# A routing-attention and bilinear-FFN kernel: weight rounding spread over the first FFN, evictions and sums on other engines, the verdict computed earlier

## The chip, the cores and the metric

The kernel runs on one core of one Trainium2 chip. The metric is the device time of one execution in microseconds (us). Before the change the median of three runs is 1273.95 us (1273.7 to 1275.91).

## The reference, cut to what matters

The inputs are `q`, `k`, `v` of shape (4, 8, 768, 64), `centroids` (8, 16, 64), the weights `moe_w_a` and `moe_w_b` (512, 1536) and `moe_w_out` (1536, 512). The weights are 64-bit floats in memory.

```python
q_assign = argmax(q_n @ c_n)            # per head: nearest of 16 centroids
k_assign = argmax(k_n @ c_n)
mask = q_assign[:, :, :, None] == k_assign[:, :, None, :]
scores = where(mask, 0.125 * q @ k.T, -1e9)
attn = softmax(scores) @ v              # (B, H, S, D) -> x of (B*S, H*D)
out = ((x @ w_a) * (x @ w_b)) @ w_out   # 3072 tokens
```

## The kernel before, in words

**Units.** Heads are taken in 16 pairs (4 batches of 4 pairs). For a pair and a half of its 768 queries (`hf`) there are six units, one for each block of 128 keys (`j` = 0 to 5); a unit is a 128x2x384 tile of scores, the middle index `a` being the head of the pair. Two units make a group, three groups a half, six a pair: 96 groups (`g`) and two more turns of the main loop (L510) to finish.

**A turn of the main loop** writes the instructions of one group in this order, and each engine works its own in that order: `score` (mask matmuls of one-hot codes L381, then scores L390 on PE; exponential L397 on ACT), `add_up` of the group before (running sums of the probabilities, L409, one head on DVE, the other on POOL), `weigh` of the group before (L420, PE), one of six preparation steps for the next pair (`prep_steps`, L347: transposes L282, centroid similarities L298, assignment L309 to L327, one-hot codes L337), rounding of weight parts (`round_w`, L219, then the load of the part after next), pieces of the FFN, and, in every third turn, `denominators` (L431: PE matmul of the finished sums, evicted by ACT L440) or, one turn later, `normalize` (L444: three reciprocals on DVE, the product with `xT` on POOL L452, and a row sum of the reciprocals on ACT L454). The turns with g a multiple of 3 hold `denominators`, those with remainder 1 `normalize`.

**Weight rounding.** 36 parts of 128x512: 24 of `wa` and `wb`, in the order of thirds of 512 columns, then 12 of `wo`. A part takes five DVE operations (L229 to L242), an addition on POOL (L245) and a last DVE operation that waits for it (L247). Before the change 9/8 parts fall on each turn, so that 29 are written by turn 25 and all by turn 31.

**The FFN** of a batch is put into a deque when its last pair is normalised (turns 25, 49, 73, 97). A batch is two blocks of 384 tokens. A block is 24 "up" pieces (L467: eight matmul records; `wa` pieces are evicted by ACT L478, `wb` pieces by a product on DVE L482) and three "down" pieces (L488, 24 records; evicted by ACT L492, stored by SP L495). A credit lets three up pieces into each turn; a down piece costs a third more, so that after three down turns one turn has none. Two blocks take 24 turns. PSUM has three buffers `m` for all preparations, denominators and pieces, two for scores and one for `O`.

**The end.** When all is written, `stat` (sums of denominators and reciprocals) gives a count of rows outside the limits (L118 to L131), all engines load it (L132) and branch: a long path L136 would recompute everything if the count were not zero.

Of the kernel before, what the change touches and what calls it, by code (L numbers as in the profile page):

```python
# [33 lines left out]
def kernel(  # L34
# [75 lines left out]

    stat = const.tile([P, 4 * B * HP], FP32, name="stat")
    with ExitStack() as fast:
        short_path(nc, tc, fast, c, cn, stat, q, k, v, moe_w_a, moe_w_b,
                   moe_w_out, out)

    fine = const.tile([P, 4 * B * HP], FP32)  # L118
    nc.vector.tensor_scalar(out=fine, in0=stat, scalar1=LIMIT, scalar2=None,
                            op0=ALU.is_le)  # L120
    least = const.tile([P, 1], FP32)
    nc.vector.tensor_reduce(out=least, in_=fine, axis=AX.X, op=ALU.min)
    far_off = const.tile([P, 1], FP32)
    nc.vector.tensor_scalar(out=far_off, in0=least, scalar1=-1.0, scalar2=1.0,
                            op0=ALU.mult, op1=ALU.add)
    n_far = const.tile([1, 1], INT32)
    with tc.tile_pool(name="ps_e", bufs=1, space=PS) as ps_e:
        ps = ps_e.tile([1, 1], FP32, name="e")
        nc.tensor.matmul(out=ps, lhsT=far_off, rhs=ones[:, 0:1], start=True,
                         stop=True)  # L130
        nc.vector.tensor_copy(out=n_far, in_=ps)  # L131
    redo = nc.values_load(n_far[0:1, 0:1], min_val=0, max_val=P,  # L132
# [5 lines left out]

def short_path(nc, tc, ctx, c, cn, stat, q, k, v, moe_w_a, moe_w_b, moe_w_out,
               out):  # L140
# [28 lines left out]
    hap = pool("hap", 2)  # L169
# [84 lines left out]
    ohs = []
    for n in range(2):
        t = zero.tile([P, 4 * 3, P], BF16, name=f"oh{n}")
        nc.gpsimd.memset(t, 0.0)
        ohs.append(t)

# [16 lines left out]
    def prep_transpose(p, i):  # L276
# [9 lines left out]
        dst = qkTs[p][:, i * 512:(i + 1) * 512]  # L286
        if i == 1:
            nc.vector.tensor_copy(out=dst, in_=ps)
        else:
            nc.scalar.copy(out=dst, in_=ps)  # L290

    def prep_sim(p):


        hp = p % HP
        ps = ps_m.tile([P, 512], FP32, name="m")
        for kq in range(4):
# [4 lines left out]
        t = simp.tile([P, HB], FP32, name="simT")  # L302
        nc.scalar.copy(out=t, in_=ps[:, 0:HB])  # L303
        sims[p] = t

    def prep_assign(p):
        ps = ps_m.tile([P, 512], FP32, name="m")
        for t in range(3):
# [6 lines left out]
        nc.vector.tensor_reduce(out=mx, in_=sim, axis=AX.X, op=ALU.max)  # L315
        eq = simp.tile([P, NG, NC], FP32, name="eq")
        nc.vector.tensor_tensor(
            out=eq, in0=sim, in1=mx[:, :, None].broadcast_to((P, NG, NC)),
            op=ALU.is_ge)
        rk = simp.tile([P, NG, NC], FP32, name="rk")  # L320
        nc.vector.tensor_tensor(
            out=rk, in0=eq, in1=rank[:, None, :].broadcast_to((P, NG, NC)),
            op=ALU.mult)
        first = small.tile([P, NG], FP32, name="first")
        nc.vector.tensor_reduce(out=first, in_=rk, axis=AX.X, op=ALU.max)
        oh = ohs[p % 2].rearrange("p n (a e) -> p (n a) e", a=2)
        nc.vector.tensor_tensor(  # L327
# [3 lines left out]
    def prep_onehot(p, w):  # L331
# [3 lines left out]
        for n in range(NJ):  # L335
            kq, t = divmod(n, 3)
            nc.tensor.transpose(out=ps[:, n * P:(n + 1) * P],  # L337
                                in_=ohs[p % 2][:, 4 * t + 2 * w + kq, :],
                                identity=identb)
# [61 lines left out]
    def add_up(u):  # L401
# [57 lines left out]

    def ffn_block(b, blk):  # L460
        box = {}
        t0 = blk * HB
# [33 lines left out]

        for f in range(NF):
            ffn.append((NCH * HB, lambda f=f: piece_a(f)))
            ffn.append((NCH * HB, lambda f=f: piece_b(f)))
        for n in range(3):  # L500
            ffn.append((NF * DM, lambda n=n: down(n)))

# [6 lines left out]

    for step in prep_steps(0):  # L510
        step()
    for g in range(NG + 2):
# [259 lines left out]
```

## Time and profile before

| | us |
|---|---|
| median of three runs | 1273.95 |
| the profiled execution | 1274.98 |
| its span, first to last instruction | 1273.1 |
| PE busy (modelled) | 1166.8 |
| DVE busy | 449.4 |
| ACT busy | 297.8 |
| POOL busy | 262.9 |

Times of rows count from the start of the span. Busy PE is modelled, since matmuls are pipelined; idle time of an engine costs only where something on the path waits for it.

### The profile page before, as it was taken

How to read it: one execution, taken by the hardware profiler on the slowest of the kernel's cores; microseconds unless marked ns; L12 is line 12 of the kernel's file. 1: busy time of each engine (PE TensorE's matmuls, PEld its weight loads, DVE VectorE, ACT ScalarE, POOL GpSimd, SP SyncE). 2: the span in 40 equal slices, each digit the busy share in tenths (PEclk: the TensorE clock that was granted, in tenths of full speed). 3: DMA queues.
4: the chain of work that ended last, by engine and by line, in shares of the span. 5: the costliest groups of instructions: out<-in, count | busy, mean ns of one | idle time of the engine just before them, and what ended most of it. 6: DMA issues, size and time to landing. Idle time of an engine off the chain costs nothing.

```text
span 1273.1 us, 11938 instructions
## 1 busy us (share of the span) xinstructions
PE 1166.8 (92%) x4723; PEld 579.6 (46%) x4723; DVE 449.4 (35%) x697; ACT 297.8 (23%) x542; POOL 262.9 (21%) x238
## 2 busy tenths in 40 slices
PE   6556555899999999999999999999999999999997
PEld 3222222355445554455445544455445544554553
DVE  5888888775312241322313140322313130110110
ACT  4223233222222322222222222222222221100000
POOL 2444343433202222221111121221111130000000
PEclk9788878899999999999999999999999999999999
DMA  6143231321020001100030001100000000000000
GB/s 169 60 120 104 67 104 66 104 75 30 8 64 17 13 1 46 41 3 11 9 78 1 13 1 54 34 13 1 9 17 1 1 1 25 1 1 25 1 1 27
DMA packets 63375, 44.92 MB, mean 35 GB/s; under 512 B 51536, under 2 KB 55632, under 8 KB 63312
## 3 DMA queue, kind: packets, MB, share of 16 engines
q1 hardware_dynamic: 63168, 44.05, 12.5%
q8 instruction: 39, 0.64, 0.2%
q14 instruction: 24, 0.20, 0.1%
q10 hardware_dynamic: 144, 0.03, 0.0%
HBM read 37.78 MB, written 6.29 MB: 35 GB/s over the span
## 4 chain that ended last, share of the span: by engine, by line
PE 82%; DVE 10%; POOL 4%; issue 3%; ACT 0%; DMA 0%; POOLq 0%; DVEq 0%; ACTq 0%
PE m L467 39%; PE m L488 20%; PE O L420 8%; PE s L390 7%; PE s L381 2%; PE m L436 2%; DVE inv L449 2%; DVE acc L409 2%; PE m L282 2%; POOL acc L409 1%; POOL wb_sb L245 1%; POOL wa_sb L245 1%; DVE wb_sb L247 1%; DVE rest L239 1%; DVE wa_sb L247 1%
## 5 line engine op out<-in xcount | busy, mean ns | idle before, releaser
L467 PE MATMUL m<-xT,wa_sb 128*128 128x384 f32 x768 | 265.6, 489 | 0.4 <-ACT simT L303 0.4
L467 PE MATMUL m<-xT,wb_sb 128*128 128x384 f32 x768 | 264.1, 487 | 0.0
L488 PE MATMUL m<-wo_sb,h 128*128 128x512 f32 x576 | 251.6, 594 | 0.0
L482 DVE TENSOR_TENSOR h<-ha,m 128x384 f32<-128x384 f32 x96 | 52.9, 553 | 403.2 <-PE m L467 403.2
L467 PEld LDWEIGHTS m<-xT,wa_sb 128*128 128x128 f32 x768 | 143.8, 190 | 108.4 <-issue 6.0
L467 PEld LDWEIGHTS m<-xT,wb_sb 128*128 128x128 f32 x768 | 144.0, 190 | 96.7 <-issue 0.6
L488 PEld LDWEIGHTS m<-wo_sb,h 128*128 128x128 f32 x576 | 108.0, 190 | 133.5 <-issue 129.4
L397 ACT ACTIVATE pt<-s 128x768 f32<-128x768 f32 x192 | 145.9, 806 | 72.3 <-issue 25.9
L390 PE MATMUL s<-qkT 64*128 64x384 f32 x768 | 154.1, 524 | 0.0
L409 POOL TENSOR_TENSOR acc<-acc,pt 128x384 f32<-128x384 f32 x128 | 141.7, 1107 | 59.5 <-ACT pt L397 53.2
L420 PE MATMUL O<-pt,v 128*64 128x384 f32 x768 | 149.8, 512 | 0.0
L478 ACT COPY ha<-m 128x384 f32<-128x384 f32 x96 | 46.0, 479 | 377.9 <-PE m L467 377.9
L452 POOL TENSOR_TENSOR xT<-xT,inv 128x384 f32<-128x384 f32 x32 | 35.7, 1114 | 440.7 <-DVE inv L449 440.7
L381 PE MATMUL s<-ohT 64*128 64x384 bf16 x384 | 51.9, 347 | 63.8 <-ACT pt L397 21.7
L409 DVE TENSOR_TENSOR acc<-acc,pt 128x384 f32<-128x384 f32 x128 | 97.5, 762 | 15.3 <-ACT pt L397 10.7
L390 PEld LDWEIGHTS s<-qkT 64*128 64x128 f32 x768 | 77.4, 203 | 35.5 <-issue 6.8
L449 DVE RECIPROCAL inv<-den 128x128 f32<-128x128 f32 x96 | 82.2, 912 | 25.9 <-ACT den L440 25.9
L420 PEld LDWEIGHTS O<-pt,v 128*64 128x64 f32 x768 | 48.1, 141 | 94.4 <-issue 90.6
L492 ACT COPY y<-m 128x512 f32<-128x512 f32 x24 | 14.1, 586 | 249.1 <-PE m L488 249.1
L409 POOL TENSOR_TENSOR acc<-pt 128x384 f32<-128x384 f32 x32 | 34.1, 1067 | 168.8 <-ACT pt L397 168.8
L381 PEld LDWEIGHTS <-ohT 64*128 64x128 bf16 x384 | 12.0, 95 | 116.8 <-issue 76.3
L436 PE MATMUL m<-acc,ones 128*64 128x384 f32 x128 | 29.1, 533 | 25.8 <-DVE acc L409 25.8
(76 smaller groups left out, 510.8 us busy)
## 6 DMA issues: line engine op xcount, KB each, us to landing
qk<-in_q_dram SPq DMA_DIRECT2D x32, 192.0 KB, 3.9
qk<-in_k_dram SPq DMA_DIRECT2D x32, 192.0 KB, 4.6
v<-in_v_dram SPq DMA_DIRECT2D x16, 384.0 KB, 4.4
raw<-in_moe_w_a_dram SPq DMA_DIRECT2D x12, 512.0 KB, 3.6
raw<-in_moe_w_b_dram SPq DMA_DIRECT2D x12, 512.0 KB, 3.6
raw<-in_moe_w_out_dram SPq DMA_DIRECT2D x12, 512.0 KB, 3.4
out_dram<-y SPq DMA_DIRECT2D x24, 256.0 KB, 2.0
csb<-in_centroids_dram ACTq DMA_DIRECT2D x1, 32.0 KB, 1.8
```

The costliest lines, as they stand in the source:

```text
L381: nc.tensor.matmul(out=s[:, a, 0:HB], lhsT=ohTs[p][r, S + j * P:S + (j + 1) * P], rhs=ohTs[p][r, hf * HB:(hf + 1) * HB], start=True, stop= ...
L390: nc.tensor.matmul(out=s[:, a, 0:HB], lhsT=qkTs[p][r, S + j * P:S + (j + 1) * P], rhs=qkTs[p][r, hf * HB:(hf + 1) * HB], start=False, stop ...
L397: nc.scalar.activation(out=pt, in_=s[:, :, 0:HB], func=AF.Exp, scale=SCALE)
L409: eng.tensor_tensor(out=acc[:, a, :], in0=probs[u - 1][:, a, :] if j == 1 else acc[:, a, :], in1=probs[u][:, a, :], op=ALU.add)
L420: nc.tensor.matmul(out=O_of[0][a * D:(a + 1) * D, 0:HB], lhsT=vs[p][:, a, j, :], rhs=probs[u][:, a, :], start=(j == 0), stop=(j == NJ - 1))
L436: nc.tensor.matmul(out=ps[a * D:(a + 1) * D, 0:HB], lhsT=ones, rhs=acc[:, a, :], start=True, stop=True)
L449: nc.vector.reciprocal(out=inv[:, n * P:(n + 1) * P], in_=den[:, n * P:(n + 1) * P])
L452: nc.gpsimd.tensor_tensor(out=x, in0=x, in1=inv, op=ALU.mult)
L467: nc.tensor.matmul(out=ps[:, 0:HB], lhsT=w_sb[:, ch, f * P:(f + 1) * P], rhs=xTs[b][:, ch, t0:t0 + HB], start=(ch == 0), stop=(ch == NCH - 1))
L478: nc.scalar.copy(out=box["a"], in_=ps[:, 0:HB])
L482: nc.vector.tensor_tensor(out=box["h"][:, f, :], in0=box["a"], in1=ps[:, 0:HB], op=ALU.mult)
L488: nc.tensor.matmul(out=ps, lhsT=box["h"][:, f, n * P:(n + 1) * P], rhs=wo_sb[:, f, :], start=(f == 0), stop=(f == NF - 1))
```

## The change

Over turns 0 to 23 only eight weight parts are rounded, one in each third turn (2, 5, ..., 23); the other 28 are written in turns 24 to 40, two or one in each (2 2 1 2 1 2 2 1 2 1 2 2 1 2 1 2 2). The FFN of the first batch is reordered to match: eight up pieces of block 0, eight of block 1, for each third of the columns, then the down pieces of both; `h` gets a second buffer. Of the first head's sums, `j` = 2 and 4 move from DVE to POOL. Two evictions of the preparation (the second of three `qkT` tiles, the second one-hot tile) move from DVE to ACT. To find the memory, `qk`, `acc`, `oh` lose their second buffer, `v` its third, and the reciprocal is taken in place in `den`, as is ACT's row sum of it. So the load of the next pair's q and k is written after the transposes, that of v two steps later. An exponential is put among the first ACT instructions. The verdict is computed after the last `normalize`, with its matmul behind the first piece of the last FFN batch; the load of the count and the branch stay at the end.

```diff
+    ce = const.tile([P, 1], FP32)
+    nc.scalar.activation(out=ce, in_=cn0, func=AF.Exp)
...
-    qkp = pool("qkp", 2)
-    vp = pool("vp", 3)
+    qkp = pool("qkp", 1)
+    vp = pool("vp", 2)
...
-    accp = pool("accp", 2)
+    accp = pool("accp", 1)
...
-    hp_ = pool("hp", 1)
+    hp_ = pool("hp", 2)
...
-        if i == 1:
-            nc.vector.tensor_copy(out=dst, in_=ps)
-        else:
-            nc.scalar.copy(out=dst, in_=ps)
+        nc.scalar.copy(out=dst, in_=ps)
...
-            nc.vector.tensor_scalar(out=dst, in0=ps[:, 0:S], scalar1=FAR,
-                                    scalar2=-FAR, op0=ALU.mult, op1=ALU.add)
+            nc.scalar.activation(out=dst, in_=ps[:, 0:S], func=AF.Identity,
+                                 scale=FAR, bias=nfar[:, 0:1])
...
-            both(lambda: load(p + 1), lambda: prep_transpose(p, 0)),
-            both(lambda: prep_transpose(p, 1), lambda: prep_transpose(p, 2)),
-            lambda: prep_sim(p),
+            lambda: prep_transpose(p, 0),
+            both(lambda: prep_transpose(p, 1), lambda: prep_transpose(p, 2),
+                 lambda: load(p + 1)),
+            both(lambda: prep_sim(p), lambda: load_v(p)),
...
-        for a, eng in ((0, nc.vector), (1, nc.gpsimd)):
+        for a in range(2):
+            eng = nc.gpsimd if a == 1 or j in (2, 4) else nc.vector
...
-        inv = denp.tile([P, HB], FP32, name="inv")
         for n in range(3):
-            nc.vector.reciprocal(out=inv[:, n * P:(n + 1) * P],
-                                 in_=den[:, n * P:(n + 1) * P])
+            part = den[:, n * P:(n + 1) * P]
+            nc.vector.reciprocal(out=part, in_=part)
         x = xTs[b][:, hp, hf * HB:(hf + 1) * HB]
-        nc.gpsimd.tensor_tensor(out=x, in0=x, in1=inv, op=ALU.mult)
+        nc.gpsimd.tensor_tensor(out=x, in0=x, in1=den, op=ALU.mult)
         n = 4 * p + 2 * hf + 1
-        nc.scalar.activation(out=den, in_=inv, func=AF.Copy,
+        nc.scalar.activation(out=den, in_=den, func=AF.Copy,
                              accum_out=stat[:, n:n + 1])
...
+    def ffn_batch(b):
+        blocks = [ffn_block(b, blk) for blk in range(2)]
+        if b == 0:
+            for n in range(3):
+                for ups, _ in blocks:
+                    ffn.extend(ups[8 * n:8 * n + 8])
+            for _, downs in blocks:
+                ffn.extend(downs)
+        else:
+            for ups, downs in blocks:
+                ffn.extend(ups + downs)
...
+    due = {}
+    for i in range(len(w_parts)):
+        due.setdefault(3 * i + 2 if i < 8 else 24 + int((i - 8) / 1.6),
+                       []).append(i)
...
-        for i in range(g * 9 // 8, (g + 1) * 9 // 8):
+        for i in due.get(g, ()):
             round_w(i)
             load_w(i + 2)
...
+    fine = zero.tile([P, 4 * NPAIR], FP32, name="fine")
+    nc.vector.tensor_scalar(out=fine, in0=stat, scalar1=LIMIT, scalar2=None,
+                            op0=ALU.is_le)
+    least = zero.tile([P, 1], FP32, name="least")
+    nc.vector.tensor_reduce(out=least, in_=fine, axis=AX.X, op=ALU.min)
+    far_off = zero.tile([P, 1], FP32, name="far_off")
+    nc.vector.tensor_scalar(out=far_off, in0=least, scalar1=-1.0, scalar2=1.0,
+                            op0=ALU.mult, op1=ALU.add)
+    ffn.popleft()[1]()
+    ps = ps_m.tile([P, 512], FP32, name="m")
+    nc.tensor.matmul(out=ps[0:1, 0:1], lhsT=far_off, rhs=ones[:, 0:1],
+                     start=True, stop=True)
+    nc.vector.tensor_copy(out=n_far, in_=ps[0:1, 0:1])
     while ffn:
         ffn.popleft()[1]()
```

## Rows read from the trace of the kernel before

**Rows 1.** Page, part 2: PE's busy tenths in 40 equal slices; its granted clock.

```profile
PE   6556555899999999999999999999999999999997
...
PEclk9788878899999999999999999999999999999999
```

**Rows 2.** Windows: stretch, its length, busy us (instructions) by engine, clock, DMA.

```profile
18.00:236.00 218.00, 128.94 (x696) 56.54 (x696) 175.26 (x260) 62.95 (x108) 92.30 (x76) 0.81 0.33 93
236.00:520.00 284.00, 283.56 (x1173) 140.39 (x1172) 104.30 (x164) 73.00 (x134) 63.36 (x56) 1.00 0.12 34
```

**Rows 3.** Timeline (start, us, engine, line, operation): first PE instructions of turns 0, 13, 14, 26, 28; a stall in turn 26.

```profile
18.13 0.82 PE L381 MATMUL s<-ohT 64*128 64x384 bf16 x4 [0.65 <-DVE ohT L344]
...
121.74 0.50 PE L381 MATMUL s<-ohT 64*128 64x384 bf16 x4
...
125.93 0.50 PE L381 MATMUL s<-ohT 64*128 64x384 bf16 x4
...
236.01 0.50 PE L381 MATMUL s<-ohT 64*128 64x384 bf16 x4
...
245.82 2.85 PE L467 MATMUL m<-xT,wa_sb 128*128 128x384 f32 x8 [0.44 <-ACT simT L303]
...
260.92 0.50 PE L381 MATMUL s<-ohT 64*128 64x384 bf16 x4
```

**Rows 4.** Timeline, 300 to 326 us: one undisturbed rounding, the next one's start; last of five assignment operations.

```profile
300.51 0.44 DVE L229 TENSOR_SCALAR wo_sb<-raw 128x512 int32<-128x512 int32 x1
...
302.94 1.38 POOL L245 TENSOR_TENSOR wo_sb<-wo_sb,rest 128x512 f32<-128x512 f32 x1 [12.72 <-DVE rest L239]
...
304.96 0.42 DVE L229 TENSOR_SCALAR wo_sb<-raw 128x512 int32<-128x512 int32 x1
...
325.96 0.56 DVE L327 TENSOR_TENSOR oh<-rk,first 128x384 bf16<-128x384 f32 x1
```

**Rows 5.** Line L409: additions on POOL and DVE, ns min/median/max.

```profile
L409 POOL TENSOR_TENSOR acc<-acc,pt x128: 985/997/1332, 30.7 to 1057.8; 128x384 f32<-128x384 f32 x128
L409 DVE TENSOR_TENSOR acc<-acc,pt x128: 494/558/1351, 32.2 to 1057.0; 128x384 f32<-128x384 f32 x128
```

**Rows 6.** Timeline around 101 us (DVE, POOL), and line L247, ns min/median/max.

```profile
101.56 1.00 POOL L409 TENSOR_TENSOR acc<-pt 128x384 f32<-128x384 f32 x1
101.64 1.47 DVE L247 SCALAR_TENSOR_TENSOR wa_sb<-ex,wa_sb 128x512 f32<-128x512 int32 x1 [1.17 <-POOL wa_sb L245]
...
L247 DVE SCALAR_TENSOR_TENSOR wo_sb<-ex,wo_sb x12: 691/1080/1474, 210.3 to 308.8; 128x512 f32<-128x512 int32 x12
```

**Rows 7.** Timeline, 1079 to 1084 us: denominators to `xT` with nothing in the way.

```profile
1079.79 0.87 PE L436 MATMUL m<-acc,ones 128*64 128x384 f32 x4
...
1081.47 2.58 DVE L449 RECIPROCAL inv<-den 128x128 f32<-128x128 f32 x3 [23.35 <-ACT den L440]
1083.27 2.74 PE L467 MATMUL m<-xT,wb_sb 128*128 128x384 f32 x8
1084.14 0.52 ACT L454 ACTIVATE den<-inv 128x384 f32<-128x384 f32 x1 [2.77 <-DVE inv L449]
1084.19 0.99 POOL L452 TENSOR_TENSOR xT<-xT,inv 128x384 f32<-128x384 f32 x1 [25.22 <-DVE inv L449]
1084.57 0.18 ACT L454 ACTIVATION_READ_ACCUMULATOR den<-inv 128x1 f32 x1
```

**Rows 8.** Timeline: the exponentials of turn 1.

```profile
23.69 1.51 ACT L397 ACTIVATE pt<-s 128x768 f32<-128x768 f32 x2 [0.50 <-PE s L390]
```

**Rows 9.** Windows around two PE waits (columns as in Rows 2).

```profile
92.00:96.00 4.00, 1.16 (x9) 0.32 (x9) 3.86 (x5) 0.30 (x1) 1.88 (x2) 1.00 0.31 120
...
103.00:113.30 10.30, 0.06 (x2) 0.10 (x1) 8.94 (x15) 2.70 (x5) 3.96 (x4) 0.73 0.19 64
```

**Rows 10.** Timeline: the last instructions of the span.

```profile
1266.57 0.58 ACT L492 COPY y<-m 128x512 f32<-128x512 f32 x1 [9.76 <-PE m L488]
1266.65 0.15 DVE L131 CAST n_far<-e 1x1 int32<-1x1 f32 x1 [29.85 <-PE e L129]
```

More of the change, by code (lines that the diff above doesn't have):

```diff
@@ L109 @@
     nc.gpsimd.memset(cTb, 0.0)
-    stat = const.tile([P, 4 * B * HP], FP32, name="stat")
+    n_far = const.tile([1, 1], INT32, name="n_far")
     with ExitStack() as fast:
-        short_path(nc, tc, fast, c, cn, stat, q, k, v, moe_w_a, moe_w_b,
+        short_path(nc, tc, fast, c, cn, n_far, q, k, v, moe_w_a, moe_w_b,
                    moe_w_out, out)
[L118 to L131, printed above, removed]
     redo = nc.values_load(n_far[0:1, 0:1], min_val=0, max_val=P,
@@ L136, with short_path @@
             long_path(nc, tc, slow, c, q, k, v, out)
-def short_path(nc, tc, ctx, c, cn, stat, q, k, v, moe_w_a, moe_w_b, moe_w_out,
+def short_path(nc, tc, ctx, c, cn, n_far, q, k, v, moe_w_a, moe_w_b, moe_w_out,
                out):
@@ L194, in load, with load_v @@
         qks[p] = t
+    def load_v(p):
+        if p >= NPAIR:
+            return
+        b, hp = divmod(p, HP)
         t = vp.tile([P, 2, NJ, D], FP32, name="v")
@@ L201, in short_path @@
     load(0)
+    load_v(0)
     WN = 512
@@ L251, in short_path @@
     load_w(1)
[L254 to L258, printed above, removed]
+    stat = zero.tile([P, 4 * NPAIR], FP32, name="stat")
+    nfar = zero.tile([P, 1], FP32, name="nfar")
+    nc.vector.memset(nfar, -FAR)
+    oh_all = zero.tile([P, 4 * 3, P], BF16, name="oh")
+    nc.gpsimd.memset(oh_all, 0.0)
     ps = ps_m.tile([P, 512], FP32, name="m")
@@ L301, in prep_sim @@
                              start=True, stop=True)
-        t = simp.tile([P, HB], FP32, name="simT")
+        t = simp.tile([P, HB], FP32, name="sim")
         nc.scalar.copy(out=t, in_=ps[:, 0:HB])
@@ L315, in prep_assign @@
         nc.vector.tensor_reduce(out=mx, in_=sim, axis=AX.X, op=ALU.max)
-        eq = simp.tile([P, NG, NC], FP32, name="eq")
+        rk = simp.tile([P, NG, NC], FP32, name="sim")
         nc.vector.tensor_tensor(
-            out=eq, in0=sim, in1=mx[:, :, None].broadcast_to((P, NG, NC)),
+            out=rk, in0=sim, in1=mx[:, :, None].broadcast_to((P, NG, NC)),
             op=ALU.is_ge)
-        rk = simp.tile([P, NG, NC], FP32, name="rk")
         nc.vector.tensor_tensor(
-            out=rk, in0=eq, in1=rank[:, None, :].broadcast_to((P, NG, NC)),
+            out=rk, in0=rk, in1=rank[:, None, :].broadcast_to((P, NG, NC)),
             op=ALU.mult)
@@ L325, in prep_assign @@
         nc.vector.tensor_reduce(out=first, in_=rk, axis=AX.X, op=ALU.max)
-        oh = ohs[p % 2].rearrange("p n (a e) -> p (n a) e", a=2)
+        oh = oh_all.rearrange("p n (a e) -> p (n a) e", a=2)
         nc.vector.tensor_tensor(
@@ L337, in prep_onehot @@
             nc.tensor.transpose(out=ps[:, n * P:(n + 1) * P],
-                                in_=ohs[p % 2][:, 4 * t + 2 * w + kq, :],
+                                in_=oh_all[:, 4 * t + 2 * w + kq, :],
                                 identity=identb)
@@ L495, in down @@
             nc.sync.dma_start(out=rows, in_=y)
[L497 to L501, printed above, removed]
+        ups = [(NCH * HB, lambda f=f, piece=piece: piece(f))
+               for f in range(NF) for piece in (piece_a, piece_b)]
+        downs = [(NF * DM, lambda n=n: down(n)) for n in range(3)]
+        return ups, downs
+    def ffn_batch(b):
[9 more added lines that the diff above has]
+                ffn.extend(ups + downs)
     GPP = UPP // 2
@@ L508, in short_path @@
     credit = 0
-    for step in prep_steps(0):
-        step()
+    due = {}
+    for i in range(len(w_parts)):
+        due.setdefault(3 * i + 2 if i < 8 else 24 + int((i - 8) / 1.6),
+                       []).append(i)
+    prep_transpose(0, 0)
+    prep_transpose(0, 1)
+    prep_transpose(0, 2)
+    load(1)
+    prep_sim(0)
+    prep_assign(0)
+    prep_onehot(0, 0)
+    prep_onehot(0, 1)
     for g in range(NG + 2):
@@ L542, in short_path @@
             if ph[1] == 1 and ph[0] % HP == HP - 1:
-                for blk in range(2):
-                    ffn_block(ph[0] // HP, blk)
+                ffn_batch(ph[0] // HP)
+    fine = zero.tile([P, 4 * NPAIR], FP32, name="fine")
[11 more added lines that the diff above has]
+    nc.vector.tensor_copy(out=n_far, in_=ps[0:1, 0:1])
     while ffn:
```

## The prediction, made before the change was run

> **What bounds the kernel now.** I read the page's slices first [rows 1]: from slice 9 on PE is busy nine tenths or more at the full clock (2.4 GHz); ahead of that it is busy five or six tenths at a clock between 0.7 and 0.9. The windows by stage say who holds it up there [rows 2]: in 18 to 236 us, turns 0 to 25, DVE is busy 175 of 218 us and PE 129; in 236 to 520 us, two blocks and more of FFN, PE is busy all the time. So only the first stretch has time to give. It lasts from the first score at 18.13 to turn 26's at 236.01, 8.4 us a turn; a turn in which nothing waits takes 4.2 (125.93 - 121.74) [rows 3]. The other end of the scale is 26 x 4.2 = 109 us instead of 218.
>
> An undisturbed rounding takes 304.96 - 300.51 = 4.45 us of DVE, waiting for POOL's 1.38 included [rows 4]. 29 parts stand in the first stretch: 129 us. After the change there are 12, eight of them one in three turns.
>
> **The change part by part.**
>
> *The port that DVE and POOL share.* POOL's addition takes 0.99 undisturbed and up to 1.33, DVE's 0.56 and up to 1.35 [rows 5]; DVE's last rounding operation takes 0.69 alone, and 1.47 when a POOL addition began just before it (101.56 to 102.56, then 0.69 more) [rows 6]. So operations of this kind go one after the other, and a sum moved from DVE to POOL occupies the common resource for 0.99 instead of 0.56. The Trainium skill, "SBUF — State Buffer", "Who interferes with whom", says that a DVE instruction with two SBUF inputs and a GpSimd one that reads SBUF exclude each other completely: the row agrees. That rule speaks against this move; without it the sum would be that of rival 1.
>
> *A half after the change, from one denominators matmul's end to the next.* POOL and DVE now hand the first head's sum back and forth, and the single `acc` ties it to the matmul. Start at 0. ACT evicts; reciprocals end at 3.4, POOL's product at 4.5 (1080.66 to 1084.05 and 1085.18) [rows 7]. Behind it on POOL: `j`=2 of both heads, to 6.5; then DVE's `j`=3 to 7.1, POOL's `j`=3 to 8.2 (port), DVE's first four rounding operations to 10.5, POOL's rounding addition to 12.0, `j`=4 to 13.0, DVE's last rounding operation to 13.7, POOL's `j`=4 to 14.7, DVE's `j`=5 to 15.3, POOL's `j`=5 to 16.3, matmul (0.87) to 17.2. In every second half the assignment (five operations of 0.56 and the gaps, 2.9) [rows 4] stands between `j`=5 and the reciprocals on DVE, of which 2.2 is covered: 17.9. PE's own work is 3 x 4.2 = 12.6 to 13.3, so it waits some 4 us at each denominators matmul. A wait of 2.8 left the clock at 1.00 in 92 to 96 us, one of 10 took it to 0.73 [rows 9]; 4 us lies between. If it falls, PE's three turns become some 16 us, still under 17.2. I take 17.2 and 17.9; bounds are PE's 13.3 and 20 (clock low, every collision lost).
>
> *First stretch.* First score 0.5 later (18.6): the second one-hot eviction now follows the first on ACT. Turn 1's exponentials end at 25.2 + 0.5 [rows 8], `j`=2 can start on POOL, and 12.6 later (17.2 - 4.5) the first denominators are done: 38.4. Seven more halves: 4 x 17.9 + 3 x 17.2 = 123.2, to 161.6; turn 25 takes 4.4: turn 26 starts at 166. Before: 236.0. Gain **70.0**; with all halves at the bounds: at 13.3 the first is done at 34.5 and turn 26 starts at 132, gain 104; at 20 at 186, gain 50.
>
> *Where the stall goes: turns 24 to 27.* Two parts each in the turns 24 and 25, which are still short. DVE from 160: parts 8, 9 to 169, `j`=1, parts 10, 11 to 178.9, reciprocals to 181.5, POOL's product to 182.7, ACT's sum of `den` to 183.4. That last one now reads and writes `den` in place and so waits for POOL's product (it did not before: L454 starts with L452 [rows 7]); on ACT turn 26's exponentials, the `simT` copy and the `wa` eviction are queued behind it, to 185.4. PE reaches the third piece of turn 26 at 166 + 4 + 2 x 2.65 = 175.3 (2.74 a piece, overlapped [rows 7]) and needs `simT`'s PSUM buffer: idle for 10. The same wait exists now, 0.44 long, at the same place (245.82) [rows 3]. In turn 27 its denominators need the buffer of a product that stands behind parts 13 and 14 on DVE, done at 205: another 5. Two turns took 260.92 - 236.01 = 24.9 before; they take some 40 now. **+15**.
>
> *Turns 28 to 40.* A turn there is 12 us of PE. DVE: 1.65 parts x 4.45 = 7.3, sum 0.6, product 0.8, reciprocals or assignment 1.3 on average, 0.8 of collisions: 10.8. It fits, but turns with two parts and reciprocals need 14, so I add **+3** (0 to 20) of waits. Weights are in time: the second third is needed from turn 31 and written by 28, the third from 36 and by 33, `wo` from 42 and by 40. PE's work is the same in any order of pieces. I also take off the 0.8 that turn 26 lost before to the same wait (245.82 against the end of its second piece, and turn 27).
>
> *Later batches.* No rounding left; PE is full [rows 1]. The added POOL sums (0.9 us a turn), ACT copies (0.3 a turn) and the wait of ACT's row sum lie beside 8 us of FFN pieces a turn: 0.
>
> *Loads.* q and k of the next pair are asked for after the transposes, on SP's queue ahead of the weight parts, and are used five turns later, over 20 us; DMA is a third busy in that stretch [rows 2]: 0. If the buffer came late by a turn, PE's transposes would wait, 1 to 2 us a pair. The early exponential takes a table load off a place where ACT waits for PE anyway: 0.
>
> *Verdict.* It moves into PE's stream behind one piece of the last batch. It needs both sums of `stat`. Before, PE starts that batch at once, at 1080.6, and its first piece ends at 1083.3 [rows 7]. The reciprocals end at 1084.05, POOL's product at 1085.18, ACT's sum 0.7 later [rows 7] at 1085.95, three small DVE operations 0.65: the verdict's matmul can run at 1086.7. All pieces are queued behind it: PE is idle for 3.5 us, **+3.5** (2 to 7, if the clock falls). At the end it takes a matmul and a cast away, to 1266.80; the last eviction runs to 1267.15 in any case [rows 10]: **-0.5** (0 to -1.5).
>
> *Sum.* -70.0 + 15 + 3 - 0.8 + 3.5 - 0.5 = -49.8. The profiled execution took 1274.98 with a span of 1273.1; 1225.2 after. The median of the runs shown is 1.0 lower: **1224**.
>
> **The rivals.**
>
> 1. *DVE and POOL do not exclude each other in this mix, and PE sets the first stretch.* Without the exclusion `j`=3 runs under POOL's, rounding starts 2 us earlier and the later sums close up: 13.9 a half, 14.6 with assignment. 38.4 becomes 35, and 4 x 14.6 + 3 x 13.9 = 100 brings turn 26 to 140: 26 less, **1198**. For it: on each engine alone the work of a half fits below PE's pace. Against: the 1.47 [rows 6].
>
> 2. *DVE becomes the bound of the rounding stretch.* In the first stretch now, everything included, a part costs 218 / 29 = 7.5 us. At this price 28 parts need 210, and the products of 15 turns 12: 222 against PE's 2 x 4.3 + 15 x 11.85 = 186, 36 lost instead of 18: **1242**. For it: POOL has more to do than now; against: in 300.51 to 304.96 the part costs 4.45 beside the FFN [rows 4].
>
> 3. *Slower: the stall repeats.* Each of the nine turns from 27 on with two parts holds a `wb` product behind both on DVE; PE has three buffers. If the parts cost 7.5 there, such a turn is 16 long instead of 12, +4, and each wait halves the clock afterwards, +3.4: 9 x 7.4 + 15 = 82 against a gain of 70: -70 + 82 + 2.2 = +14, **1288**. It decides from some 6 us lost in each of the nine turns. For it: two thirds of the rounding moves beside work that is on the path; against: now one part beside FFN costs PE nothing.
>
> 4. *The change does not do what it says*: the row sum or the denominators of the first stretch still wait for something else on DVE, so that halves take 27 us as now. Then about 1274 + 20: counted with 3.
>
> **How the numbers follow.** Forecast 0.66, rival 1 0.14, rival 2 0.15, rivals 3 and 4 0.05. The bounds of the forecast alone: 1190 (halves at 13.3) to 1244 (halves at 20), the turns 28 to 40 up to 17 worse and the verdict up to 3.5. The range of 8 in 10 takes in most of rivals 1 and 2: **1194 to 1252**. A difference of 0.2% (2.5 us) is what can be told from none. Faster 0.95, same 0.01, slower 0.04.
>
> **What would show it.** Turn 26's first score near 166 us (forecast), 140 (rival 1) or above 200 (rival 4). PE's waits ahead of L436 in the first stretch, some 4 us, released by the sums on POOL or DVE. DVE's share there down from 80% to between 55% and 70%, POOL's up from 42% to some 55%. One PE wait of about 10 us in turn 26 released by ACT, another of about 5 before turn 28; few later (many: rival 2 or 3). A wait of 3.5 us ahead of the verdict's matmul after the last normalisation. The forecast is wrong if halves are not 17 to 18 us apart, or if turns 28 to 41 are longer than before by more than 20 in all.

## The result, and the profile after

The changed kernel takes **1226.09 us** (median of four executions, 1223.04 to 1227.35) against 1274.47 of the kernel before beside it: a ratio of 0.9616, 95% interval 0.9596 to 0.9636. The forecast was 1224. The profiled execution of it took 1223.04 with a span of 1221.3, that is 51.9 less than the profiled one of before.

The page of the changed kernel, part 2 (40 slices; busy tenths of PE, DVE and POOL, PE's granted clock), which answers [rows 1]:

```profile
PE   6978869999989999999999999999999998999998
...
DVE  3777777677671202223112321313022221100100
...
POOL 2665643344432212222112222204122220000000
PEclk8998979999999999999999999999999999999999
```

The weak slices end after slice 6 of 30.5 us each instead of after slice 8 of 31.8 us each, and the clock's digit is 7 or 8 on three slices instead of seven.

The windows of the changed kernel by stage (stretch, length, busy us and instructions of PE, PEld, DVE, ACT, POOL, then granted clock, DMA share, GB/s): first score to turn 26, turn 26 to turn 50. They answer [rows 2]:

```profile
18.00:156.50 138.50, 118.37 (x696) 51.12 (x696) 97.94 (x121) 67.01 (x117) 82.05 (x72) 0.94 0.25 68
156.50:465.50 309.00, 289.73 (x1181) 143.07 (x1180) 166.96 (x257) 77.91 (x143) 108.04 (x93) 0.97 0.22 64
```

The first stretch is 79.5 shorter (218.0 to 138.5). PE is idle there for 20.1 instead of 89.1, which is 69.0 of it; the other 10.6 are PE's own busy time, 128.94 to 118.37 for the same 696 matmul records, as its clock is 0.94 instead of 0.81. In the next stretch PE has 19.3 us of idle time where it had 0.4.

With the first score of turns 26 and 50, the start of the last FFN batch and the end as marks, the whole difference splits up:

| stretch | before | after | difference | forecast |
|---|---|---|---|---|
| to turn 26's first score | 236.0 | 156.5 | -79.5 | -70.0 |
| turns 26 to 49 | 285.2 | 309.1 | +23.9 | +17.2 (15 + 3 - 0.8) |
| turn 50 to the last batch | 559.4 | 559.4 | 0 | 0 |
| verdict: last batch's first piece to its third | 5.27 | 10.49 | +5.2 | +3.5 |
| the rest, with the end | | | -1.5 | -0.5 |
| sum | | | -51.9 | -49.8 |

**One half of the first stretch.** Timeline of the changed kernel from one denominators matmul (L427, L436 before) to the next (start, us, engine, line, operation, count; in brackets the idle time before it and its releaser):

```profile
117.25 2.30 PE L427 MATMUL m<-acc,ones 128*64 128x384 f32 x4 [2.04 <-DVE acc L400]
...
119.65 0.56 DVE L400 TENSOR_TENSOR acc<-pt 128x384 f32<-128x384 f32 x1 [2.54 <-PE m L427]
...
120.26 2.58 DVE L440 RECIPROCAL den<-den 128x128 f32<-128x128 f32 x3
...
122.98 1.00 POOL L442 TENSOR_TENSOR xT<-xT,den 128x384 f32<-128x384 f32 x1 [1.93 <-ACT pt L387]
...
123.95 3.23 POOL L400 TENSOR_TENSOR acc<-acc,pt 128x384 f32<-128x384 f32 x3
...
124.98 1.34 DVE L400 TENSOR_TENSOR acc<-acc,pt 128x384 f32<-128x384 f32 x1 [2.13 <-POOL acc L400]
...
126.24 1.22 DVE L222 TENSOR_SCALAR wa_sb<-raw 128x512 int32<-128x512 int32 x1
...
129.45 1.39 POOL L238 TENSOR_TENSOR wa_sb<-wa_sb,rest 128x512 f32<-128x512 f32 x1 [2.28 <-DVE rest L232]
...
130.80 3.66 POOL L400 TENSOR_TENSOR acc<-acc,pt 128x384 f32<-128x384 f32 x3
130.88 1.47 DVE L240 SCALAR_TENSOR_TENSOR wa_sb<-ex,wa_sb 128x512 f32<-128x512 int32 x1 [1.17 <-POOL wa_sb L238]
...
132.27 1.34 DVE L400 TENSOR_TENSOR acc<-acc,pt 128x384 f32<-128x384 f32 x1
...
133.67 0.86 PE L427 MATMUL m<-acc,ones 128*64 128x384 f32 x2 [1.72 <-DVE acc L400]
```

This is the chain of the forecast, link by link: reciprocals, POOL's product, sums handed back and forth, a rounding part in the middle, the last sum, the matmul. DVE's sums take 1.34 here. Line L400 (ns min, median, max of one), the answer to [rows 5]:

```profile
L400 POOL TENSOR_TENSOR acc<-acc,pt x192: 981/1000/1447, 24.3 to 1002.8; 128x384 f32<-128x384 f32 x192
...
L400 DVE TENSOR_TENSOR acc<-acc,pt x64: 545/1336/1354, 25.3 to 1001.8; 128x384 f32<-128x384 f32 x64
```

Before, a DVE sum that met a POOL one was the exception (median 558, maximum 1351); now the median is 1336: with three of four sums of a pair of blocks on POOL, 46 of the 64 sums that are left on DVE take more than 1200 ns, and all 16 of the first stretch.

**Turn 26.** Timeline of the changed kernel, the chain that ends in PE's longest wait:

```profile
156.52 0.50 PE L371 MATMUL s<-ohT 64*128 64x384 bf16 x4
...
170.39 2.57 DVE L440 RECIPROCAL den<-den 128x128 f32<-128x128 f32 x3
173.11 0.99 POOL L442 TENSOR_TENSOR xT<-xT,den 128x384 f32<-128x384 f32 x1 [3.36 <-DVE den L440]
...
174.13 0.52 ACT L444 ACTIVATE den<-den 128x384 f32<-128x384 f32 x1 [16.86 <-POOL xT L442]
...
174.65 1.49 ACT L387 ACTIVATE pt<-s 128x768 f32<-128x768 f32 x2
...
176.03 0.48 ACT L293 COPY sim<-m 128x384 f32<-128x384 f32 x1
...
176.56 5.49 PE L458 MATMUL m<-xT,wa_sb 128*128 128x384 f32 x8 [10.67 <-ACT sim L293]
```

The reciprocals stand on DVE behind four rounding parts, ACT's in-place row sum L444 waits 16.86 for POOL's product, and PE waits 10.67 for a copy that is queued behind it on ACT; the piece after that takes 5.49 instead of 2.74, at a granted clock of 0.50 (176.50 to 181.90). Turn 26 takes 25.5 us (156.52 to 181.99) instead of 12.6.

**Verdict.** Timeline of the changed kernel around it (PE, and ACT's row sum):

```profile
1025.08 2.85 PE L458 MATMUL m<-xT,wa_sb 128*128 128x384 f32 x8
...
1029.65 0.52 ACT L444 ACTIVATE den<-den 128x384 f32<-128x384 f32 x1 [3.78 <-POOL xT L442]
...
1031.08 0.19 PE L572 MATMUL m<-ones,far_off 128*1 128x1 f32 x2 [3.15 <-DVE far_off L568]
...
1031.20 4.54 PE L458 MATMUL m<-xT,wb_sb 128*128 128x384 f32 x8
...
1035.57 2.74 PE L458 MATMUL m<-xT,wa_sb 128*128 128x384 f32 x8
```

The wait is 3.15, and the piece behind it 4.54 instead of the 2.74 of [rows 7].

**The end.** The last eviction in the changed kernel, which answers [rows 10]:

```profile
1216.30 0.59 ACT L483 COPY y<-m 128x512 f32<-128x512 f32 x1 [9.76 <-PE m L479]
```

No matmul and no cast stand beside it any more; 5.0 us of the span lie behind its start, 6.5 before the change.

### The profile page after: what moved, and what is told of

Read it like the earlier page. It is cut to its first block, busy times and chain, and to the rows that moved or that the text cites. A ratio compares the mean times of both kernels' runs of the same rounds, so it can differ in the third digit from the quotient of the medians.

```text
span 1221.3 us, 11866 instructions
## 1 busy us (share of the span) xinstructions
PE 1162.9 (95%) x4723; PEld 576.6 (47%) x4723; DVE 413.5 (34%) x602; ACT 317.8 (26%) x575; POOL 326.0 (27%) x301
## 3 DMA queue, kind: packets, MB, share of 16 engines
q1 hardware_dynamic: 63168, 44.05, 12.6%
## 4 chain that ended last, share of the span: by engine, by line
PE 80%; DVE 8%; issue 5%; POOL 5%; ACT 1%; DMA 0%; POOLq 0%; DVEq 0%; ACTq 0%
PE m L458 37%; PE m L479 20%; PE O L411 8%; PE s L380 7%; PE s L371 2%; POOL acc L400 2%; DVE den L440 2%; PE m L427 2%; PE m L275 2%; DVE acc L400 2%; POOL wb_sb L238 1%; POOL wa_sb L238 1%; PE m L288 1%; POOL wo_sb L238 1%; DVE rest L232 1%
## 5 line engine op out<-in xcount | busy, mean ns | idle before, releaser
L400 POOL TENSOR_TENSOR acc<-acc,pt 128x384 f32<-128x384 f32 x192 | 204.4, 1080 | 52.4 <-ACT pt L387 47.4
L411 PE MATMUL O<-pt,v 128*64 128x384 f32 x768 | 145.8, 501 | 0.0
L380 PE MATMUL s<-qkT 64*128 64x384 f32 x768 | 143.9, 495 | 0.0
L400 POOL TENSOR_TENSOR acc<-pt 128x384 f32<-128x384 f32 x32 | 39.5, 1235 | 353.0 <-PE m L427 333.4
L400 DVE TENSOR_TENSOR acc<-acc,pt 128x384 f32<-128x384 f32 x64 | 74.1, 1157 | 126.7 <-POOL acc L400 126.7
L440 DVE RECIPROCAL den<-den 128x128 f32<-128x128 f32 x96 | 82.3, 913 | 23.4 <-ACT den L431 22.8
L380 PEld LDWEIGHTS s<-qkT 64*128 64x128 f32 x768 | 72.7, 193 | 33.2 <-issue 3.0
L442 POOL TENSOR_TENSOR xT<-xT,den 128x384 f32<-128x384 f32 x32 | 31.9, 997 | 190.2 <-DVE den L440 188.3
L400 DVE TENSOR_TENSOR acc<-pt 128x384 f32<-128x384 f32 x32 | 18.6, 580 | 142.0 <-PE m L427 135.1
L427 PE MATMUL m<-acc,ones 128*64 128x384 f32 x128 | 35.5, 528 | 12.2 <-DVE acc L400 12.2
```

The source lines that it names most:

```text
L380: nc.tensor.matmul(out=s[:, a, 0:HB], lhsT=qkTs[p][r, S + j * P:S + (j + 1) * P], rhs=qkTs[p][r, hf * HB:(hf + 1) * HB], start=False, stop ...
L400: eng.tensor_tensor(out=acc[:, a, :], in0=probs[u - 1][:, a, :] if j == 1 else acc[:, a, :], in1=probs[u][:, a, :], op=ALU.add)
L411: nc.tensor.matmul(out=O_of[0][a * D:(a + 1) * D, 0:HB], lhsT=vs[p][:, a, j, :], rhs=probs[u][:, a, :], start=(j == 0), stop=(j == NJ - 1))
L427: nc.tensor.matmul(out=ps[a * D:(a + 1) * D, 0:HB], lhsT=ones, rhs=acc[:, a, :], start=True, stop=True)
L440: nc.vector.reciprocal(out=part, in_=part)
```

## The experiments

All are edits of the changed kernel (called "the change" here); each line of the table gives its median, its ratio to the kernel before and, of its profiled execution, the start of turn 26, the length of turns 26 to 49, and the last batch from its first piece to the end of its last matmul (185.9 before the change). From turn 50 to the last batch each of them has 559.4.

| kernel | us | ratio (interval) | turn 26 at | turns 26-49 | last batch |
|---|---|---|---|---|---|
| the change | 1226.1 | 0.9616 (0.9596-0.9636) | 156.5 | 309.1 | 191.1 |
| e1 sums back | 1215.5 | 0.9527 (0.9500-0.9553) | 150.5 | 306.6 | 192.4 |
| e2 rounding back | 1278.1 | 1.0027 (1.0016-1.0039) | 237.0 | 284.5 | 191.1 |
| e3 verdict later | 1219.3 | 0.9567 (0.9551-0.9583) | 159.8 | 309.2 | 186.2 |
| e4 late parts later | 1217.9 | 0.9564 (0.9548-0.9580) | 157.3 | 302.1 | 191.1 |
| e5 evictions back | 1238.0 | 0.9718 (0.9702-0.9734) | 172.6 | 307.0 | 191.1 |
| e6 row sum apart | 1221.6 | 0.9581 (0.9565-0.9597) | 159.5 | 305.9 | 190.1 |
| e7 three edits | 1204.6 | 0.9451 (0.9435-0.9467) | 152.5 | 299.8 | 186.2 |
| e8 early parts later | 1219.6 | 0.9575 (0.9559-0.9591) | 163.1 | 302.3 | 186.2 |
| e9 four edits | 1199.8 | 0.9411 (0.9393-0.9430) | 151.1 | 295.8 | 186.2 |
| e10 mixed | 1192.8 | 0.9357 (0.9340-0.9374) | 143.9 | 296.3 | 186.2 |
| e11 one-hot back | 1222.1 | 0.9582 (0.9565-0.9599) | 158.9 | 306.7 | 191.1 |
| e12 spread alone | 1229.5 | 0.9656 (0.9640-0.9672) | 170.7 | 299.2 | 190.2 |

The first stretch of e3 has the same instructions as that of the change, and turn 26 starts at 159.8 in one and 156.5 in the other: 3 us there are the difference between two executions and are read as nothing.

**e1, the sums back on DVE.**

```diff
-            eng = nc.gpsimd if a == 1 or j in (2, 4) else nc.vector
+            eng = nc.gpsimd if a == 1 else nc.vector
```

> All five sums of the first head go back to DVE, everything else is as after the change. Theory A (the serial chain through POOL and the shared port sets the halves, so the moved sums lengthen them): a half from denominators to denominators falls from 15.7 and 17.1 us to 13.3 to 14.5, turn 26 starts at 132 to 140 instead of 156.5, the rounding turns lose up to 3 more since DVE has 0.4 us more in a turn; 1204 to 1212 us in all. Rival B (DVE was what held the first stretch, and the moved sums are part of the gain): halves of 17 us or more, 1226 to 1235.

It is 10.6 faster than the change, a little less than theory A had, and turn 26 starts at 150.5 and not at 132 to 140. Halves without assignment are 14.5 instead of 15.7 to 16.4, those with it 16.4 to 17.8 beside 17.1 to 17.5; turns 26 to 49 are 2.5 shorter and not up to 3 longer. Timeline of e1, sums and product of one half (POOL, DVE):

```profile
117.45 1.12 POOL L442 TENSOR_TENSOR xT<-xT,den 128x384 f32<-128x384 f32 x1 [1.93 <-DVE den L440]
118.54 2.45 POOL L400 TENSOR_TENSOR acc<-acc,pt 128x384 f32<-128x384 f32 x2
...
124.15 2.40 POOL L400 TENSOR_TENSOR acc<-acc,pt 128x384 f32<-128x384 f32 x2
...
125.63 2.00 DVE L400 TENSOR_TENSOR acc<-acc,pt 128x384 f32<-128x384 f32 x2
```

POOL has two additions in a row instead of three, and DVE's two take 2.00 together, where one took 1.34. The median of DVE's L400 is 558 ns again. So moving these sums to POOL costs time in this kernel, some 10 us, and none of the gain is theirs. How much of it is the port and how much the longer chain of additions on POOL, the run doesn't tell.

**e2, the rounding at its old pace**, 9/8 parts in each turn; all else as in the change.

```diff
-        due.setdefault(3 * i + 2 if i < 8 else 24 + int((i - 8) / 1.6),
-                       []).append(i)
+        due.setdefault(-(-8 * (i + 1) // 9) - 1, []).append(i)
```

> The weight parts are written again at 9/8 a turn from turn 0 on, everything else is as after the change (FFN order, sums, evictions, verdict). Theory A (the spread rounding carries the gain): turn 26 at 200 to 225 us, the waits in turns 26 to 41 (24 us) vanish, 1250 to 1270 us. Rival B (the moved sums and evictions carry it): turn 26 before 175, at most 1235 us.

Turn 26 starts at 237.0, as before the change (236.0), and turns 26 to 49 take 284.5, as before (285.2). The whole gain, and the whole stall behind it, belong to the new due times of the parts. What the moves could have brought is not seen, because the chain through the reciprocals is still behind two parts on DVE. Timeline of e2, DVE, POOL, ACT and PE at one change of pair:

```profile
160.87 2.57 DVE L440 RECIPROCAL den<-den 128x128 f32<-128x128 f32 x3
...
163.58 0.99 POOL L442 TENSOR_TENSOR xT<-xT,den 128x384 f32<-128x384 f32 x1 [3.35 <-DVE den L440]
...
164.61 0.52 ACT L444 ACTIVATE den<-den 128x384 f32<-128x384 f32 x1 [16.61 <-POOL xT L442]
...
168.16 0.82 PE L371 MATMUL s<-ohT 64*128 64x384 bf16 x4 [15.79 <-ACT ohT L333]
```

PE waits 15.79 for a one-hot eviction that is queued on ACT behind the in-place row sum. The waits at the four changes of pair are 9.7 to 15.8; before the change they were 7.9 to 13.0, and the trace has them end with an instruction of DVE. It was expected to be faster than it is; that the in-place row sum takes the eviction along was not thought of. This is read from the rows: no run takes the two apart here.

**e3, the verdict behind four pieces instead of one.**

```diff
-    ffn.popleft()[1]()
+    for _ in range(4):
+        ffn.popleft()[1]()
```

> The verdict's matmul stands behind four pieces of the last batch instead of one. Theory A (PE waits there for the last row sum, 3.15 us, and then runs a piece at half the clock, 1.8): no wait, 4 to 5 us less, about 1221. Rival B (something else waits there and the time is only moved): 1226, no difference.

The last batch falls from 191.1 to 186.2 (before the change 185.9), and the wait ahead of the verdict's matmul is gone. The 5 us of the verdict lie where the step put them.

**e4, the late parts begun in turn 26 instead of 24.**

```diff
-        due.setdefault(3 * i + 2 if i < 8 else 24 + int((i - 8) / 1.6),
+        due.setdefault(3 * i + 2 if i < 8 else 26 + int((i - 8) / 1.75),
```

> The 28 parts are written in turns 26 to 41 (1.75 a turn) instead of 24 to 40, so the two short turns without FFN hold none. Theory A (the 10.7 us wait in turn 26 is four parts queued ahead of the last reciprocals): turn 26 takes 13 to 14 instead of 25.5 us, the later waits grow from 11 to 13 to 20; 1215 to 1224. Rival B (DVE's total between turns 24 and 41 sets the loss, wherever the parts stand): the waits sum up to 24 again, 1226.

Turn 26 now takes 11.9 us: no part stands any more ahead of the reciprocals that it waits for. Part of the stall comes back further on (turn 29 has a wait of 3.22 and 5.5 us more than before the change, turn 41 5.7 more), and turns 26 to 49 are 7.0 shorter in all.

**e5, both evictions back on DVE; e11, only the one-hot one.**

```diff
-        nc.scalar.copy(out=dst, in_=ps)
+        if i == 1:
+            nc.vector.tensor_copy(out=dst, in_=ps)
+        else:
+            nc.scalar.copy(out=dst, in_=ps)
...
-            nc.scalar.activation(out=dst, in_=ps[:, 0:S], func=AF.Identity,
-                                 scale=FAR, bias=nfar[:, 0:1])
+            nc.vector.tensor_scalar(out=dst, in0=ps[:, 0:S], scalar1=FAR,
+                                    scalar2=-FAR, op0=ALU.mult, op1=ALU.add)
```

(e11 has the second hunk alone.)

> The two evictions of the preparation go back from ACT to DVE, all else as after the change. Theory A (the two one-hot evictions in a row on ACT are what PE waits for at each change of pair, 1.4 to 2.1 us): that wait falls under 0.7, the first stretch is 3 to 6 us shorter, the rounding turns lose 1 to 2 more since DVE has 1.2 us more in a pair; 1220 to 1226. Rival B (the first stretch is set by the chain of the sums alone, a wait less at the change of pair is a wait more at the next denominators): turn 26 stays at 156, 1226 to 1229.

e5 is 12 slower than the change, more than either theory had. The waits at a change of pair do fall, from 1.4 to 2.1 down to 0.7 to 1.4, but every second half is now 20.4 to 21.9. Timeline of e5 in such a half (POOL's product has L445 there):

```profile
94.29 0.69 DVE L281 COPY qkT<-m 128x512 f32<-128x512 f32 x1 [3.51 <-PE m L275]
...
94.89 2.56 DVE L443 RECIPROCAL den<-den 128x128 f32<-128x128 f32 x3
...
97.60 1.00 POOL L445 TENSOR_TENSOR xT<-xT,den 128x384 f32<-128x384 f32 x1 [5.97 <-DVE den L443]
```

The copy of `qkT` itself takes 0.69. But it stands ahead of the reciprocals in DVE's order and waits 3.51 for PE's transposes, and the reciprocals, the product and all sums wait with it: the product begins 9.8 behind the start of the denominators matmul (87.82) instead of 5.7 (117.25 to 122.98 above).

> Of the two evictions moved to ACT only the one-hot one goes back to DVE. Theory A (the 12 us that both cost on DVE come from the copy of qkT, which waits for PE's transposes ahead of the reciprocals): 1222 to 1228, turn 26 at 155 to 158, the wait at a change of pair 0.7 instead of 1.4 to 2.1. Rival B (the one-hot eviction carries it, as it stands ahead of the sums that the denominators need): 1234 to 1240, turn 26 at 168 to 173.

e11 tells the two apart: turn 26 at 158.9, no half of 20 us. The one-hot eviction costs nothing on DVE: e11 is 4.0 faster than the change, which the two intervals don't quite tell apart, 2.4 of it in turns 26 to 49. The copy of `qkT` carries the whole loss, 15.8 from e11 to e5.

**e6, a tile of its own for the output of ACT's row sum**, so that it doesn't wait for POOL's product.

```diff
-        nc.scalar.activation(out=den, in_=den, func=AF.Copy,
+        junk = denp.tile([P, HB], BF16, name="junk")
+        nc.scalar.activation(out=junk, in_=den, func=AF.Copy,
```

> ACT's row sum of the reciprocals writes a tile of its own instead of den, so it waits for the reciprocals and no longer for POOL's product. Theory A (ACT, and the exponentials and copies queued behind that row sum, hold PE in turns 26 and 41): the wait in turn 26 falls from 10.7 to 9.6, the one in turn 41 from 3.2 to 2.2, the one at the verdict by 1; 1222 to 1224. Rival B (PE is held by DVE's products and sums there, ACT comes on top of nothing): no difference.

4.5 faster in the medians (1.4 between the two profiled executions): the wait in turn 26 is 8.28 instead of 10.67, one in turn 41 2.15 instead of 3.23, the verdict's 2.32 instead of 3.15. In e3, which has the change's instructions up to there, the wait in turn 26 is 9.18. So these waits lose 0.8 to 1.1, about the length of POOL's product, 0.99, and the one in turn 26 between 0.9 and 2.4.

**e7, e1, e3 and e4 together; e9, e6 added to them.** The diffs are those above.

> Sums back on DVE, parts from turn 26 on at 1.75 a turn, and the verdict behind four pieces, together. Alone they took 10.6, 8.2 and 6.8 us off. Theory A (they work at different places: the chain of a half, the short turns 24 and 25, the verdict): about 1200, turn 26 at 150, no wait of 10. Rival B (sums on DVE and a denser rounding use up the same DVE time in turns 26 to 41): 1205 to 1212, waits of 20 to 28 there.

> The three edits together gave 1204.56; this adds the tile of its own for ACT's row sum, so that no exponential stands behind POOL's product. Theory A (that wait lies on the path in turn 29 and 41 and ahead of the verdict, as alone, where it was worth 4.5): 1200 to 1202, turn 29 shorter than 17.26 by 1 to 2 us. Rival B (with the late parts begun two turns later, DVE's products of the pieces hold PE there, not ACT's sum): 1203 to 1206, turn 29 as long as with the three edits.

The single gains (10.6, 6.8 and 8.2) add up to 25.6, and 21.5 is measured. From turn 26 on nothing is missing: turns 26 to 49 are 2.5 shorter in e1, 7.0 in e4 and 9.4 here, and the last batch is 4.9 shorter in e3 and here. So rival B does not hold. Turns 29 and 41 take 17.3 and 18.3 against 11.7 each before, but 17.3 and 17.5 in e4 alone: that is the price of the later parts, not of the sums. The 4 us that are missing are not found in any stretch behind turn 26; 3 us at its start are what executions of the same instructions differ by. e9 gives another 4.8; turn 29 falls to 14.5 and turn 41 to 17.1, so ACT's wait for the product was on the path there, as theory A had it.

**e8, e7 with the eight early parts one turn later, behind the denominators; e10, e9 with every second of them one turn later.**

```diff
-        due.setdefault(3 * i + 2 if i < 8 else 26 + int((i - 8) / 1.75),
+        due.setdefault(3 * i + 3 if i < 8 else 26 + int((i - 8) / 1.75),
```

(e10: `3 * i + 2 + i % 2`.)

> As the run with three edits, but the eight early parts are written one turn later, in turns 3, 6, ..., 24, so that DVE rounds behind the last sums of a half instead of ahead of them. Theory A (what PE waits for at the denominators is a rounding queued in front of the last sums on DVE): halves of 13.3 to 15 instead of 14.5 and 16.4 us, turn 26 at 138 to 145, 5 to 10 us less than the three edits. Rival B (the total of DVE and POOL work of a half sets it, in any order): halves of 15.5 on average, no difference.

It is 15.0 slower than e7. Halves are 12.6 and 21.7 to 22.3 in turn. 12.6 is PE's own pace (3 x 4.2). Timeline of e8 in a long one, at a change of pair (DVE, POOL, ACT, PE):

```profile
74.46 1.47 DVE L240 SCALAR_TENSOR_TENSOR wa_sb<-ex,wa_sb 128x512 f32<-128x512 int32 x1 [1.16 <-POOL wa_sb L238]
...
76.32 2.56 DVE L440 RECIPROCAL den<-den 128x128 f32<-128x128 f32 x3
...
80.17 0.52 ACT L444 ACTIVATE den<-den 128x384 f32<-128x384 f32 x1 [9.01 <-POOL xT L442]
...
82.75 0.92 ACT L333 ACTIVATE ohT<-m,nfar 128x768 bf16<-128x768 bf16 x1
...
83.73 0.82 PE L371 MATMUL s<-ohT 64*128 64x384 bf16 x4 [8.15 <-ACT ohT L333]
```

There the part stands between the five assignment operations and the reciprocals on DVE, so the product, ACT's row sum and the one-hot eviction behind it are late, and PE waits 8.15. Theory A held for the halves without assignment and fell for the others.

> The four edits, and of the eight early parts every second one a turn later (turns 6, 12, 18, 24 instead of 5, 11, 17, 23), the others as in the change. Theory A (a rounding part costs PE a wait in a half only where it stands between a sum and the matmul that needs it, or ahead of the reciprocals; with parts in these turns neither): halves at 14.5 and at 12.6 to 13.5 instead of 14.5 and 17.4, turn 26 at 134 to 140, 1184 to 1192. Rival B (DVE and POOL together have a half's work of about 16 us, the order only moves the wait): the mean half stays at 15.5 to 16, turn 26 at 148 to 152, 1198 to 1203.

So e10 leaves the parts of the halves with assignment where they were. It is the fastest of all, 1192.8 us: 33.3 below the change. Turn 26 starts at 143.9, 7.2 ahead of e9's but short of theory A's 134 to 140: halves are 14.0 to 16.8, 15.0 in the mean. The longest has a wait of 4.21 ahead of its matmul; there the part of turn 12 ends on DVE 3.5 behind the start of the denominators (81.71 against 78.2), and the reciprocals with it, where the part of turn 6 ends 1.1 behind and the half takes 14.6. DVE's and POOL's work in a half still counts, and its place as well; neither theory is right alone.

**e12, the spread of the rounding alone:** sums (e1) and both evictions (e5) back on DVE, and the row sum's own tile (e6).

> Of the change only the new due times of the weight parts with the FFN order that goes with them, the single buffers and the verdict are left: sums and both evictions are back on DVE, and ACT's row sum has a tile of its own. Theory A (the effects of the single undoings add up: -10.6 for the sums, +12 for the evictions, -4.5 for the row sum, so the two moves off DVE as a pair are worth nothing beside the spread): 1219 to 1226, turn 26 at 158 to 168. Rival B (with sums and evictions both on DVE, DVE becomes the bound of a half and the moves are worth something as a pair): 1232 to 1245, turn 26 above 172.

It lies between the two theories: 1229.5, turn 26 at 170.7, every second half 19.8, with the `qkT` copy ahead of the reciprocals (a wait of 4.22 for the transposes) as in e5. Against e6, which differs by the moves only, it is 7.9 slower. So of the change's 48 us the spread brings 44 without the moves (1229.5 against 1273.6 of the kernel before beside it), with the verdict's loss, the FFN order, the single buffers, the early exponential and the row sum's own tile in it. What the evictions gain is mostly eaten by what the sums and the in-place row sum cost. The single undoings do not add up: 12 less 10.6 would make the two moves worth 1.4, and they are worth 7.9.

The single buffers and the early exponential were not undone by themselves. In the half shown above DVE's first sum of the next half (119.65) waits 2.54 for the denominators matmul, which reads the one `acc`; what a second buffer would be worth is not shown.

## Why the prediction was right

The median lies 2.1 above the forecast and the profiled execution 2.1 below its own (51.9 less instead of 49.8), with larger errors of both signs in the steps: -9.5 in the first stretch, -1.4 in turns 26 and 27, +8.1 in turns 28 to 41, +1.7 at the verdict, -1.0 at the end. That the spread of the rounding carries the gain, and that its stall comes back behind turn 24, was right; that the total is so near is in part luck.

**The first stretch** (forecast -70.0, measured -79.5; other executions of the same instructions give up to 3 less). The mechanism is shown: e2 has the old pace of rounding and turn 26 at 237.0, as the kernel before at 236.0. The term was mis-sized mostly in one place. From the end of POOL's product to the start of the next denominators matmul the forecast has 11.8 us; in the half shown above it is 9.7 (123.98 to 133.67). Two links were taken too long: up to the end of POOL's rounding addition 6.9 instead of 7.5 have passed (130.84), and the matmul of the first head doesn't wait for POOL's last addition of the second head, which runs on to 134.46. The matmul in turn takes 1.6 to 2.4 instead of 0.87, since its second half waits for that addition. Halves are 15.7 to 17.5, 16.7 in the mean over seven, instead of 17.6: 6.5 us. The first denominators end at 35.8 instead of 38.4: another 2.6. By one of its own signs, halves of 17 to 18 us, the forecast was off: three of seven are shorter. DVE's share of the stretch is 71% and POOL's 59%, where 55 to 70 and some 55 were written.

**The port.** That DVE's and POOL's additions get in each other's way was in the sum: the L400 rows (1336 instead of 558) bear it out, and e1's 10.6 us fit it. The Trainium skill, "SBUF — State Buffer", "Who interferes with whom", lets a DVE instruction with two SBUF inputs and a GpSimd one that reads SBUF exclude each other, and so spoke against moving the sums; the L400 rows agree with it. Rival 1, built on its absence, is refuted by these rows, and turn 26 starts at 156.5, not at 140.

**The evictions** were costed at nothing, with a start 0.5 later, and that step failed: e5 shows them worth 12 us together, and e5 against e11 the copy of `qkT` alone 15.8. What was overlooked is not its 0.69 us but its place: DVE works in order, and that copy waits for PE ahead of the reciprocals. At each change of pair a wait of 1.4 to 2.1 is left of the 7.9 to 13.0, now released by ACT's eviction; the forecast had none there. The 4 us of wait it put ahead of each denominators matmul are 0.7 to 2.4.

**Turns 24 to 27** (forecast +15: 10 in turn 26, 5 in turn 27). The wait in turn 26 came out as written, the same instructions in the same order, 10.67 (9.18 in e3); e4 and e6 confirm it from two sides. The clock behind it was left out: turn 26 is 12.9 longer than before, 2.7 of that in the slow piece. The 5 in turn 27 did not come: that turn takes 12.28 (12.32 before). The forecast has its denominators wait for the buffer of a product that stands behind the two parts on DVE. Timeline of the changed kernel, PE and DVE:

```profile
193.47 0.87 PE L427 MATMUL m<-acc,ones 128*64 128x384 f32 x4
...
198.34 1.00 DVE L473 TENSOR_TENSOR h<-ha,m 128x384 f32<-128x384 f32 x2
```

The matmul starts without a wait, 4.9 ahead of the products, so it doesn't need their buffer; before the change it was so too (260.12 and 261.51). The parts were also done at 198.4 and not at 205: DVE had been idle for 2.12 ahead of 185.83, while the forecast had it still working off its backlog. The two turns together are 12.8 longer, where the sum had 15 - 0.8, because the slow piece stands in for more than half of the 5.

**Turns 28 to 41** (forecast +3). Four turns are longer, 30, 33, 36 and 41, by 1.4, 4.05, 1.8 and 3.85 us (36 against e2, which has the new order of pieces and no stall). Two of them, with the granted clock in the windows right behind (the columns as above):

```profile
260.40 4.54 PE L458 MATMUL m<-xT,wb_sb 128*128 128x384 f32 x8 [2.10 <-DVE h L473]
...
365.08 2.85 PE L458 MATMUL m<-xT,wa_sb 128*128 128x384 f32 x8 [3.23 <-ACT ohT L331]
```

```profile
260.40:263.00 2.60, 2.60 (x5) 1.48 (x6) 2.50 (x5) 0.00 (x0) 1.52 (x2) 0.56 0.00 2
...
365.10:367.70 2.60, 2.60 (x8) 1.60 (x9) 0.00 (x0) 0.73 (x1) 2.52 (x4) 1.00 0.00 0
```

So 11.1 in these turns instead of 5 + 3 in turns 27 to 40. The mechanism of rival 3 is there, a product that stands behind two parts on DVE, but in three turns and not nine. Rival 2 would have needed 36 lost; it is 23.9 over turns 26 to 49.

**The verdict** (forecast 3.5, bounds 2 to 7): the wait is 3.15, and the clock behind it falls, which only the upper bound held: 5.2. **The end**: -1.5 where -0.5 was taken, at its bound.

## What to carry to other kernels

Work on an in-order engine is worth what stands behind it: the 0.69 us copy that waits for another engine ahead of the reciprocals cost 15.8 us, and a rounding part cost nothing or 8 us of PE's wait according to its turn. When work is spread off a critical stretch, leave the last turns ahead of the next stage free of it, and ask for each wait which it adds what is queued behind the waiting instruction. And before a sum is moved to another engine, ask whether the two hold each other up: here it was better to leave it.

## What the runs showed of the hardware

The clock after a wait doesn't follow from the wait's length in these rows: behind the 2.10 us wait at 260.40 it is 0.56, which is nearly the lower level of 1.2 GHz with a piece of 4.54 us, and behind the 3.23 us wait at 365.08 it is 1.00, 2.4 GHz, with a piece of 2.85. Ahead of the first PE had done masks, scores, the weighing and a transposition of 0.55; ahead of the second a whole FFN piece of 2.80. What decides between them stays open.

One operand doesn't free a DVE operation from POOL: L222, which reads a single tile, stands 36 times in the trace of the changed kernel. Of these 18 took 1.21 to 1.23, each beside an addition of POOL begun 0.26 to 0.39 ahead of it (126.24 in the half shown above); the other 18, with no work on POOL beside them, took 0.41 to 0.42 (0.44 in [rows 4]). L235, of the same form, begins 0.16 ahead of POOL's addition L238, runs beside it and takes 0.42 in all 36: the one that began first was not held up.
